# Attention and token mixer on one core: a rewrite around token halves, with four-byte transposes of fp16 pairs and four-quadrant values products

## The chip, the cores and the metric

The kernel runs on 1 core of one Trainium2 chip. The metric is the device time of one execution in microseconds (us). Most figures are medians of a few executions; a profile is one profiled execution, whose "span" runs from the first to the last instruction. An execution counts as "slow" when it is over 1.5% above the fastest of the same kernel. Ratios below are the mean time of one kernel's fast runs over the mean of the other's fast runs of the same rounds, so they are not quite the ratios of the medians quoted beside them. One "point" is 1% of the time of the kernel before, about 1.94 us.

## The reference

Inputs q, k, v are 8 batches x 8 heads x 576 tokens x 64, fp32. Each batch goes through three parts:

```
coarse:  q_d, k_d, v_d = means over 4 tokens;  softmax(q_d k_d' / 8) v_d, each row repeated 4 times
local:   softmax over |i-j| < 4 of (q k' / 8), times v
x     =  coarse + local, heads side by side: 576 x 512
mixer:   wq = x w_q ; wk = x w_k ; M2 = wk' x / 8 ; mixed = wq M2 ; out = relu(mixed) w_out
```

The kernel never forms the 576 x 576 matrix of the mixer: it computes M2 (64 x 512) first.

## The kernel before

The batches are software-pipelined. One iteration runs the parts of three batches in a fixed order; TensorE works through them while ScalarE and VectorE empty PSUM, GpSimd casts and sums, and SyncE issues every load and store. PSUM is a ring of three 2-bank tiles (`ps`) and one of two 1-bank tiles (`psm`). Names in the profile: `pv` values means, `psc` local scores, `pav` local scores times values, `pm` M2, `pmx` and `pmr` the product with M2, `pcs` coarse scores, `pca` coarse times values, `pq`, `pk`, `pr` transposes of q, k and their last rows, `po` the output product, `pol` its last 64 rows, `px`, `pod` transposes of x and the coarse result, `pw`, `pws`, `pwk` the projections and their rearrangements.

```
def load_v(b):                                    # 10 loads of 128 KB per batch
    v32 = ... [128, NW, H, D] fp32
    for n in range(NW):                           # NW = 5 windows, two of 64 tokens each
        for c in range(2):
            sp.dma_start(v32[64*c:64*c+64, n],
                         _ap(v[b], K0[2*n+c]*D, [[D, 64], [S*D, H], [1, D]]))

def tr(key, dst):                                 # q and k: 16 two-byte transposes each
    for j in range(NP):
        for f in range(4):
            pe.transpose(p_[...], t_[:, f, 2*j:2*j+2, :], id16)
    evac(dst, ..., p_...)                         # 128 x 2048 fp16, ScalarE

def av(n):                                        # two quadrants: token half c -> rows and columns 64c
    for s_ in range(2):
        for hh in range(NP):
            for c in range(2):
                pe.matmul(p_[64*c:64*c+64, ...], E[64*c:64*c+64, ...], v16[64*c:64*c+64, n, h, :],
                          tile_position=(64*c, 64*c))
    dve.reciprocal(rz[:, n], ...); dve.tensor_tensor(x_, p_, rz, op=ALU.mult)

def m2():                                         # 7 matmuls of 512 columns
    ...
    evac("M2", M2[0:64], p_[0:64], scale=s_mix)   # ScalarE; rows 64 to 127 stay zero

def mx(i):                                        # two 2-bank tiles, and mxr for the last 64 tokens
    for rr in range(2):
        r = 2*i + rr
        pe.matmul(p_[:, rr, :], M2[:, 128*r:128*r+128], wT[:, 0:512], start=True, stop=True)
    evac("mx%d" % i, ..., p_, relu=True)

ORDER = [ ... (0, "av0"), (-1, "m2"), (0, "av3"), (0, "score2"), (0, "av1"), (-1, "mx0"), (0, "av2"),
    (0, "cs0"), (-1, "mx1"), (0, "cs1"), (0, "av4"), ..., (-1, "mxr"), (1, "tq"), (0, "ca0"),
    (2, "load_v"), (-1, "og0"), (0, "ca1"), (1, "tk"), (1, "tr"), (-1, "ol"), (0, "xt0"), (0, "xt1"), ... ]
# ... cut: casts, sums, scores, coarse attention, projections, stores
```

The softmax here doesn't subtract the row's maximum and nothing guards it: scores larger than these inputs give would overflow.

## Time and profile before

| | before |
|---|---|
| time, 2 runs | 193.12 us median (192.64 and 193.6) |
| span of the profile, mean granted TensorE clock | 192.7 us, 0.950 |
| steady period (one batch) | 19.30 us, clock 1.00 |
| TensorE busy in it | 18.52 us |
| VectorE, ScalarE, GpSimd busy in it | 12.3, 13.2, 13.6 us |

The page of the profile. The first line is busy time and share by engine; PEclk is the granted TensorE clock in tenths of full speed (9 stands for 90% or more), in 40 slices of the span; DMA is the busy share of the 16 DMA engines in tenths.

```profile
span 192.7 us, 6374 instructions
PE 155.5 (81%) x2720; PEld 104.0 (54%) x2720; DVE 114.8 (60%) x286; ACT 110.7 (57%) x140; POOL 107.7 (56%) x122
...
PEclk9999555999789999999999999999999999999997
DMA  5999999899899799967999899969996943004215
...
q1 hardware_dynamic: 73920, 40.12, 81.7%
```

From the eighth slice on the clock is whole but for three slices (0.7 or 0.8), and the DMA engines are busy almost throughout until the loads end. A steady batch, from one values product to the next (columns: length of the stretch, busy us and instructions of each engine, clock, DMA share, GB/s):

```profile
core 0: us, PE busy (x) PEld busy (x) DVE busy (x) ACT busy (x) POOL busy (x), PEclk, DMA share, GB/s
...
102.04:121.34 19.30, 18.52 (x341) 12.43 (x340) 12.32 (x29) 13.22 (x18) 13.58 (x13) 1.00 0.92 245
```

TensorE is busy for 96% of it. The timeline of TensorE in that batch (start, length, engine, output and inputs, shape, count; in brackets the idle time ahead and who ended it):

```profile
102.04 0.39 PE L27 MATMUL pv<-v_1_149,P_153 128*32 128x512 f16 x1
...
105.07 0.39 PE L27 MATMUL pm_2266<-od_1955,wk_221 112*128 112x512 f16 x1
...
107.93 0.59 PE L27 MATMUL pmx<-wT_219,M_1_223 128*128 128x512 f16 x2 [0.41 <-ACT E_0_135 L27]
...
109.09 0.30 PE L27 MATMUL pcs<-qd,kd_127 64*128 64x144 f16 x4 [0.20 <-DVE x_2330 L27]
...
110.62 0.45 PE L27 MATMUL pav<-v_1_149,E_0_135 64*64 64x65 f16 x16 [0.17 <-ACT Ec_2356 L27]
...
111.20 1.05 PE L27 MATMUL pq_2408<-id_67,q_2110 128*128 128x128 f16 x16
...
112.55 1.89 PE L27 MATMUL po<-wo_91,rmx_227 128*128 128x512 f16 x8
...
114.75 1.06 PE L27 MATMUL pk_2480<-id_67,k_2111 128*128 128x128 f16 x16
115.64 0.39 PE L27 MATMUL pr<-id_67,r_2112 128*128 128x128 f16 x4
```

Three marks cut the batch into stretches: `pv` to `pm` 3.03 us, `pm` to `pq` 6.13, `pq` to the next `pv` (121.34) 10.14. The idle gaps are short: 0.41, 0.20 and 0.17 us. The next view is SyncE, which holds the issuing queue of all loads and stores (length of an issue, not of its transfer):

```profile
69.95 0.44 SPq L27 DMA_DIRECT2D q_1237<-in_q_dram  x1
70.89 1.27 SPq L27 DMA_DIRECT2D k_1238<-in_k_dram  x1
72.26 2.40 SPq L27 DMA_DIRECT2D r_1239<-in_q_dram  x1
74.71 2.23 SPq L27 DMA_DIRECT2D r_1239<-in_k_dram  x1
77.04 11.80 SPq L27 DMA_DIRECT2D v_1497<-in_v_dram  x10
88.94 0.57 SPq L27 DMA_DIRECT2D out_dram<-os  x1
```

The 17 issues of a batch take about 20 us.

### The profile page before, as it was taken

How to read it: one execution, taken by the hardware profiler on the slowest of the kernel's cores; microseconds unless marked ns; L12 is line 12 of the kernel's file. 1: busy time of each engine (PE TensorE's matmuls, PEld its weight loads, DVE VectorE, ACT ScalarE, POOL GpSimd, SP SyncE). 2: the span in 40 equal slices, each digit the busy share in tenths (PEclk: the TensorE clock that was granted, in tenths of full speed). 3: DMA queues.
4: the chain of work that ended last, by engine and by line, in shares of the span. 5: the costliest groups of instructions: out<-in, count | busy, mean ns of one | idle time of the engine just before them, and what ended most of it. 6: DMA issues, size and time to landing. Idle time of an engine off the chain costs nothing.

```text
span 192.7 us, 6374 instructions
## 1 busy us (share of the span) xinstructions
PE 155.5 (81%) x2720; PEld 104.0 (54%) x2720; DVE 114.8 (60%) x286; ACT 110.7 (57%) x140; POOL 107.7 (56%) x122
## 2 busy tenths in 40 slices
PE   0034448885899989998999899989998999898790
PEld 0034227853576647664776476647764776465330
DVE  6263978754646566656665666566656665685220
ACT  2037134954565767576757675767576757633422
POOL 5701991099748991895479547954895476000000
PEclk9999555999789999999999999999999999999997
DMA  5999999899899799967999899969996943004215
GB/s 175 314 187 215 348 290 162 191 354 175 175 319 218 174 264 294 263 137 201 278 323 156 184 280 346 187 154 296 330 215 154 300 146 112 3 3 153 93 57 188
DMA packets 74027, 40.54 MB, mean 210 GB/s; under 512 B 52432, under 2 KB 68880, under 8 KB 74000
## 3 DMA queue, kind: packets, MB, share of 16 engines
q1 hardware_dynamic: 73920, 40.12, 81.7%
q8 instruction: 21, 0.34, 0.7%
q14 instruction: 6, 0.05, 0.1%
q10 hardware_dynamic: 80, 0.03, 0.1%
HBM read 30.67 MB, written 9.44 MB: 208 GB/s over the span
## 4 chain that ended last, share of the span: by engine, by line
PE 68%; DVE 17%; ACT 7%; issue 4%; POOL 2%; ACTq 0%; DVEq 0%
PE po L27 15%; PE psc L27 6%; PE pav L27 5%; PE pw L27 4%; PE px L27 4%; PE pca L27 4%; PE pol L27 4%; DVE kd_127 L27 3%; PE pv L27 2%; PE pcs L27 2%; ACT kT L27 2%; PE pod L27 2%; DVE rz L27 1%; PE pws L27 1%; PE pwd L27 1%
## 5 line engine op out<-in xcount | busy, mean ns | idle before, releaser
L27 ACT COPY os<-po 128x1024 f32<-128x1024 f32 x16 | 16.2, 1012 | 14.7 <-issue 8.3
L27 DVE RECIPROCAL rz<-pav 128x8 f32<-128x8 f32 x40 | 8.1, 204 | 13.4 <-PE pav L27 13.4
L27 PE MATMUL po<-wo_91,rmx_227 128*128 128x512 f16 x64 | 15.3, 379 | 0.6 <-ACT rmx_227 L27 0.6
L27 PE MATMUL po<-wo_91,rmx_212 128*128 128x512 f16 x64 | 15.1, 379 | 0.0
L27 DVE COPY xT<-px 128x928 f16<-128x928 f16 (+1 forms) x32 | 13.8, 451 | 0.6
L27 PE MATMUL pq_236<-id_67,q_229 128*128 128x128 f16 x16 | 1.9, 312 | 12.6 <-DVE q_229 L27 12.6
L27 PE MATMUL psc<-id_67,neg 64*128 64x232 f16 (+1 forms) x80 | 9.4, 278 | 2.8 <-DVE vblk_201 L27 2.8
L27 PEld LDWEIGHTS <-rmx_227 128*128 128x128 f16 x80 | 7.2, 98 | 8.1 <-ACT rmx_227 L27 0.7
L27 PE MATMUL psc<-qT,kT 64*64 64x58 f16 (+1 forms) x640 | 11.4, 198 | 0.0
L27 PEld LDWEIGHTS <-rmx_212 128*128 128x128 f16 x80 | 7.2, 98 | 6.6
L27 DVE RECIPROCAL rc<-pca 128x8 f32<-128x8 f32 (+1 forms) x16 | 3.4, 211 | 11.8 <-PE pca L27 11.8
L27 PEld LDWEIGHTS <-wqk_90 128*128 128x128 f16 x96 | 8.3, 98 | 3.7 <-issue 0.9
L27 PEld LDWEIGHTS <-kT 64*64 64x64 f16 x640 | 8.7, 113 | 2.1 <-issue 2.1
L27 ACT COPY odT<-pod 128x448 f16<-128x448 f16 (+1 forms) x16 | 5.6, 402 | 6.3 <-PE pod L27 6.3
L27 PE MATMUL pw<-xT,wqk_90 128*128 128x288 f16 x64 | 9.2, 286 | 0.0
L27 PEld LDWEIGHTS <-q_229 128*128 128x128 f16 x16 | 1.6, 146 | 12.6 <-DVE q_229 L27 12.6
L27 POOL CAST v_0_147<-v_79 128x2560 f16<-128x2560 f32 x1 | 3.1, 3129 | 9.3 <-DMA w_92<-in_moe_w_k_dram 9.3
L27 DVE TENSOR_TENSOR wT_219<-pw,wTd 128x576 f16<-128x576 f32 x4 | 3.0, 758 | 8.6 <-ACT wTd L27 8.6
L27 DVE COPY ol<-pol 64x512 f32<-64x512 f32 x8 | 5.5, 682 | 4.3 <-PE pol L27 4.3
L27 DVE TENSOR_TENSOR wT_204<-pw,wTd 128x576 f16<-128x576 f32 x4 | 3.0, 758 | 8.0 <-ACT wTd L27 6.6
L27 DVE TENSOR_SCALAR rmx_227<-pmx 128x1024 f16<-128x1024 f32 x4 | 4.9, 1224 | 4.1 <-PE pmx L27 4.1
L27 POOL CAST v_1_149<-v_255 128x2560 f16<-128x2560 f32 x1 | 2.3, 2323 | 8.6 <-DMA v_255<-in_v_dram 8.6
(542 smaller groups left out, 540.9 us busy)
## 6 DMA issues: line engine op xcount, KB each, us to landing
out_dram<-os SPq DMA_DIRECT2D x16, 512.0 KB, 4.4
v_79<-in_v_dram SPq DMA_DIRECT2D x10, 128.0 KB, 4.6
v_255<-in_v_dram SPq DMA_DIRECT2D x10, 128.0 KB, 5.4
v_583<-in_v_dram SPq DMA_DIRECT2D x10, 128.0 KB, 3.5
v_1024<-in_v_dram SPq DMA_DIRECT2D x10, 128.0 KB, 4.4
v_1497<-in_v_dram SPq DMA_DIRECT2D x10, 128.0 KB, 3.6
v_1970<-in_v_dram SPq DMA_DIRECT2D x10, 128.0 KB, 4.3
v_2443<-in_v_dram SPq DMA_DIRECT2D x10, 128.0 KB, 3.4
```

The source lines that it names most:

```text
L27: return lambda *a, **k: self._tc.keep_in_program_order(f_(*a, **k))
```

## The change

The intent is to take work from TensorE. Tokens are laid out by halves (288 + 288). q and k come in as 18 whole rows per partition, are cast into fp16 pairs, and a pair is transposed as one fp32 element: 18 transposes instead of 36. v is split by head parity on the partition halves, so that the local values product can use all four 64 x 64 quadrants of the array (sixteen of its matmuls took 0.38 us before and about 0.25 after). M2 is copied to both partition halves so that the product with it runs on two row tiles at once, in four pieces. The last 64 rows of two batches share one output product. Two things less visible change as well: the fp16 copy of v has two buffers instead of three, and the two `rmx` tiles become one with two halves.

```diff
 def load_qk(b):
-    # q, k: [[4*D, 128], [S*D, H], [1, 4*D]] each, and two loads of the last 64 rows
+    for src, nm in ((q[b], "q32"), (k[b], "k32")):
+        sp.dma_start(t, _ap(src, 0, [[18*D, 128], [4*S*D, 2], [1, 18*D]]))
 def load_v(b):
     for n in range(NW):
         for c in range(2):
-            sp.dma_start(v32[64*c:64*c+64, n], _ap(v[b], K0[2*n+c]*D, [[D, 64], [S*D, H], [1, D]]))
+            for g in range(2):
+                sp.dma_start(v32[64*g:64*g+64, n, c],
+                             _ap(v[b], (g*S + K0[n][c])*D, [[D, 64], [2*S*D, 4], [1, D]]))
 def tr(key, dst):
-    (16 transposes of 128x128 fp16)
+    t_ = g_[key].bitcast(FP32)
+    for f in range(8):
+        pe.transpose(p_[...], t_[:, f].rearrange("p u e s -> p (u e s)"), id32)
 def av(n):
+    for hq in range(4):
+        for g, c in ((0, 0), (1, 1), (0, 1), (1, 0)):
+            pe.matmul(p_[64*c:64*c+64, g, ...], E[64*g:64*g+64, ...], v16[64*g:64*g+64, n, c, hq, :],
+                      start=True, stop=True, tile_position=(64*g, 64*c))
 def m2():
     evac("M2", M2[0:64], p_[0:64], scale=s_mix)
+    dve.tensor_copy(M2[64:128], M2[0:64])
-def mx(i): two 2-bank tiles of two 512-column matmuls, and mxr
+def mx(r): four 2-bank tiles
+    for c in range(2):
+        pe.matmul(p_[:, c, 0:HS], M2[64*c:64*c+64, 128*r:128*r+128], wT[64*c:64*c+64, c, 0:HS], ...)
 def ol():
+    if b % 2 == 0: return
+    (128 rows: the last 64 of one batch and the first 64 of the next)
-ORDER: ... av1, mx0, av2, cs0, mx1, cs1, av4, mxr, tq ...
+ORDER: ... av1, mx0, mx1, av2, cs0, mx2, cs1, av4, mx3, tq ...
... cut: constants, casts, sums, masks, scores, coarse attention, projections
```

## The prediction

> **What bounds it now.** Steady iterations (one batch each) last 19.30 us; the busy times by stretch give PE 18.52, POOL 13.6, ACT 13.2, DVE 12.3 us in each, the DMA engines 0.86-0.93 of it, clock 1.00. The chain of waits is nearly all PE there: 16 output matmuls (po) 3.46 us, M2 (pm) 1.62, 36 two-byte transposes of q, k and remainder 2.07, x transposes 1.12, local AV 80 matmuls about 2.0 (25-28 ns each), mx+mxr 1.1, pw 0.98, pca 0.94, pol 0.86, pcs 0.7, pv 0.66. About 0.9 us is DVE and ACT work it waits for (x, Ec). Before that PE waits 12.6 us for the first q cast, then behind DVE's 7.6 us of kd/kdt adds; steady state starts near 60 us, and the last batch drains from 176 us.
>
> **What changes per iteration on PE** (estimates from the trace).
> - AV on four quadrants: the scores already run so, 32 in 0.45 us, 14 ns each. 80 x 14 = 1.2: -0.8.
> - mx with K=64, two row tiles together: four times 288 columns, 0.5 instead of 1.1: -0.6.
> - ol once for two batches: -0.43. cs: -0.3. vd on 64x32 tiles: -0.25.
> - 18 four-byte transposes for 36 two-byte ones at 56-60 ns. [...] I guess 60-110 ns each, 1.1-2.0 us: 0 to -1. No fp32 transpose stands in this trace.
> PE work falls from 18.4 to 15-16 us.
>
> **Other engines.** ACT: qT/kT eviction 1.86 us for 2048 two-byte elements becomes 1024 four-byte ones, about 1.0 like os (1.01): -1.5 in all, 11.8. DVE about even, 11.8 (merged od, xT; half of ol; plus a copy of M2 and mx in two pieces). POOL: casts 2 x (2 x 1152) elements into 4-byte-strided halves, about 4.4-5.5 us (was 1.9+1.9+0.6); kd adds 160 instead of 116 elements: 14-15 us. DMA: q, k as 4608 B runs instead of 1024 and 256 B; v stays at 256 B packets in 20 half-size loads; 17.5 to about 16 us.
>
> **Critical path.** Not all 3 us come home. (a) Between av0 and ca0 PE will hold 4.5-5 us of work against DVE's 5 x 0.84 for x plus two mx evictions, about 5.8, with three PSUM buffers: DVE-bound, some 1 us lost. (b) A loop on POOL: remainder eviction -> sums -> q/k casts -> tq -> ca/og0 -> tk, tr -> eviction. Before it is 11.4 + 5.3 us with 2.6 slack; after about 12.5 + 4.7 = 17.2. I predict the loop closes: iteration about 17.2 us, PE busy some 90%.
> Seven such iterations: -15. Start: fewer constants ahead of the q cast, shorter qT/kT evictions, less kd: -5. Tail: -1. Sum: 193.1 - 21 = 172 us; I say 173, range 164 to 184. Faster by over 2%: 0.91; within 2%: 0.06; slower: 0.03.
>
> **What shows it.** Period 16.5-17.8 us; AV 15 ns apart; fp32 transposes at 60-110 ns; qT eviction near 1.0 us; PE waiting for q casts by POOL at tq, or for DVE's x tiles at PSUM buffers; ACT and DVE near 11.8 us per period; DMA share still about 0.9; first transpose near 10-11 us.
>
> **What would make it wrong.** [...] strided casts on POOL or DVE at half rate (POOL loop to 19+, little gain); 20 v loads holding the issuing queue so that v's cast comes late; or, the other way, POOL's casts not binding and the period reaching 15.7 (result near 162).

Two passages on fp32 transposes, which no trace of this case showed, are cut: a reason given ahead of the guess of 60 to 110 ns, and the first of the ways to be wrong. The guess rests on no measurement but the 56 to 60 ns of the two-byte transposes; measured afterwards: 109 ns apart, 113 on average. The sum: 15, 5 and 1 us are the 21, and 193.1 - 21 = 172; the "0 to -1" us an iteration in it rests on that guess.

## The result, and the profile after

| | before | after |
|---|---|---|
| time, 2 runs each | 193.12 us | 226.94 us (225.48 and 228.39) |
| ratio of fast runs, 95% interval | | 1.1743 [1.1549, 1.1937] |
| span, mean clock | 192.7 us, 0.950 | 223.8 us, 0.847 |
| steady period | 19.30 us | 22.2 to 25.5 us |

It became slower by 17%, where 10% faster was predicted. The page after:

```profile
span 223.8 us, 6572 instructions
PE 167.9 (75%) x2816; PEld 110.6 (49%) x2816; DVE 107.0 (48%) x260; ACT 99.1 (44%) x141; POOL 115.3 (52%) x112
...
PEclk9996558757889967997699959995899699958999
DMA  6946993597379349933998389836992474002206
...
q1 hardware_dynamic: 54464, 40.12, 62.5%
...
q8 instruction: 22, 0.36, 0.7%
```

Every engine's share fell, and so did that of the DMA engines (81.7 to 62.5%) at the same 40.12 MB: no engine has too much work, the kernel waits. The clock falls again and again all along. By stretches of TensorE's timeline the span grew 7.5 us up to the third values product (63.44 to 70.93), 20.3 us over the next five batches (96.50 to 116.77), and 3.3 us after them. One of the five batches, and then its middle in pieces of 3.4 us (columns as before):

```profile
94.45:117.41 22.96, 20.24 (x351) 13.33 (x350) 11.67 (x25) 11.58 (x18) 14.38 (x12) 0.85 0.68 194
...
99.80:103.20 3.40, 1.84 (x76) 1.12 (x65) 2.80 (x6) 1.55 (x3) 3.40 (x3) 1.00 0.31 68
103.20:106.60 3.40, 2.50 (x29) 1.69 (x30) 2.40 (x6) 2.17 (x3) 0.32 (x1) 0.61 0.44 99
106.60:110.00 3.40, 3.40 (x20) 2.10 (x19) 0.96 (x3) 1.01 (x1) 1.69 (x1) 0.50 0.89 297
```

TensorE stands idle for 1.56 of 3.40 us, and directly afterwards its clock is granted at one half. TensorE's timeline in the same batch:

```profile
94.45 0.53 PE L27 MATMUL pv<-v,Pm 64*32 64x260 f16 x24
...
97.96 0.60 PE L27 MATMUL pm<-od,wk 128*128 128x512 f16 x2
...
100.75 0.42 PE L27 MATMUL pmx<-wT,M 64*128 64x288 f16 x2 [0.60 <-ACT E L27]
101.83 0.30 PE L27 MATMUL pmx<-wT,M 64*128 64x288 f16 x2 [0.67 <-DVE x L27]
...
102.68 0.52 PE L27 MATMUL pcs<-qd,kd 64*128 64x168 f16 x12 [0.29 <-DVE x L27]
...
104.18 0.46 PE L27 MATMUL pcs<-qd,kd 64*128 64x168 f16 x4 [0.54 <-DVE x L27]
...
105.58 1.94 PE L27 MATMUL pq<-id,q 128*128 128x128 f32 x8 [0.22 <-ACT Ec L27]
...
108.21 3.15 PE L27 MATMUL po<-wo,rmx 128*128 128x512 f16 x8
...
111.66 1.07 PE L27 MATMUL pk<-id,k 128*128 128x128 f32 x8
112.57 0.27 PE L27 MATMUL pr<-id,q 128*128 128x128 f32 x1
```

The stretches are now 3.51, 7.62 and 11.83 us (were 3.03, 6.13, 10.14). In the middle one the gaps are 0.60, 0.67, 0.29, 0.54 and 0.22. In the last one `po` takes 3.15 us instead of 1.89: that is the half clock, not more work. And at full clock the eight fp32 transposes `pk` take 0.91 us to the start of `pr`, where the sixteen fp16 ones took 0.89: no gain. VectorE in the middle stretch:

```profile
100.30 0.52 DVE L27 COPY M<-M 64x512 f16<-64x512 f16 x1 [1.29 <-ACT M L27]
100.85 0.21 DVE L27 RECIPROCAL rz<-pav 128x8 f32<-128x8 f32 x1
101.09 0.69 DVE L27 TENSOR_TENSOR x<-pav,rz 128x512 f16<-128x512 f32 x1
```

VectorE takes its instructions in program order here. It stands 1.29 us until ScalarE has written M2, copies it, and only then begins on the next local result (TensorE had it ready at 99.89), whose PSUM tile TensorE needs back: the results behind the copy wait for something that has nothing to do with them. Last, SyncE's queue from the start, and in a steady batch:

```profile
1.80 17.00 SPq L27 DMA_DIRECT2D v<-in_v_dram  x20
...
22.51 20.08 SPq L27 DMA_DIRECT2D v<-in_v_dram  x20
...
110.48 19.31 SPq L27 DMA_DIRECT2D v<-in_v_dram  x20
```

The twenty loads of 64 KB take 17 to 21 us to issue in a batch, about 0.85 to 1.04 us each; the ten of 128 KB took 9.4 to 11.8. TensorE's wait for the cast of v (us in total, times, longest), before and after:

```profile
PE pv L27 <- POOL v_0_147 L27: 5.2, 1, 5.2
...
PE pv L27 <- POOL v L27: 14.3, 2, 8.6
```

Before, it was 5.2 us, once. Now the first two batches stand 8.6 and 5.6 us for the cast of v, which waits for the last load of v. In the later batches TensorE does not wait for v.

### The profile page after: what moved, and what is told of

Read it like the earlier page. It is cut to its first block, busy times and chain, and to the rows that moved or that the text cites. A ratio compares the mean times of both kernels' runs of the same rounds, so it can differ in the third digit from the quotient of the medians.

```text
span 223.8 us, 6572 instructions
## 1 busy us (share of the span) xinstructions
PE 167.9 (75%) x2816; PEld 110.6 (49%) x2816; DVE 107.0 (48%) x260; ACT 99.1 (44%) x141; POOL 115.3 (52%) x112
## 3 DMA queue, kind: packets, MB, share of 16 engines
q1 hardware_dynamic: 54464, 40.12, 62.5%
## 5 line engine op out<-in xcount | busy, mean ns | idle before, releaser
L27 POOL CAST v<-v 128x2560 f16<-128x2560 f32 x8 | 18.6, 2322 | 54.6 <-DMA v<-in_v_dram 38.5
L27 PE MATMUL po<-wo,rmx 128*128 128x512 f16 x128 | 36.1, 432 | 0.1
L27 DVE TENSOR_TENSOR x<-pav,rz 128x512 f16<-128x512 f32 x40 | 27.7, 691 | 1.4
L27 POOL TENSOR_TENSOR sum<-qT 128x1152 f32<-128x1152 f16 x8 | 16.8, 2106 | 18.2 <-ACT qT L27 17.8
L27 PE MATMUL pq<-id,q 128*128 128x128 f32 x64 | 15.6, 425 | 12.3 <-DVE q L27 10.7
L27 PEld LDWEIGHTS <-rmx 128*128 128x128 f16 x144 | 14.7, 109 | 17.2 <-issue 6.9
L27 ACT ACTIVATE E<-psc 128x928 f16<-128x928 f32 (+1 forms) x24 | 19.4, 806 | 6.4 <-PE psc L27 5.7
L27 POOL CAST q<-q 128x1152 f16<-128x1152 f32 x14 | 20.2, 1488 | 0.0
L27 POOL CAST k<-k 128x1152 f16<-128x1152 f32 x14 | 20.2, 1485 | 0.0
L27 PEld LDWEIGHTS pq<-id,q 128*128 128x128 f32 x64 | 12.5, 224 | 14.0 <-DVE q L27 10.7
L27 PE MATMUL pv<-v,Pm 64*32 64x260 f16 (+1 forms) x192 | 4.9, 286 | 14.3 <-POOL v L27 14.3
L27 POOL TENSOR_TENSOR sum<-kT 128x1152 f32<-128x1152 f16 x7 | 14.7, 2106 | 0.5
```

The source lines that it names most:

```text
L27: return lambda *a, **k: self._tc.keep_in_program_order(f_(*a, **k))
```

## The experiments

Theory Q: the issuing queue costs the most. Theory G: the copy of M2 on VectorE, and the fourfold product with M2, open the gaps in the middle stretch. Theory C: the gaps bring the half clock, which costs more than the gaps. Rival: TensorE's new work (fp32 transposes, many narrow matmuls) is simply longer. Kernels are named for what they change; "m2pe", "mx3", "fill" and "vpool2" are explained where they first occur. Edits are to the kernel after, unless said.

| kernel | result | median us | ratio to before, fast runs [95%] |
|---|---|---|---|
| copy_late | right | 229.69 | 1.1821 [1.1733, 1.1909] |
| m2pe | right | 221.9 | 1.1406 [1.1316, 1.1496] |
| v10wrong | wrong | 210.27 | 1.0834 [1.0761, 1.0908] |
| bv20 (kernel before) | right | 233.0 | 1.1996 [1.1881, 1.2111] |
| v10wrong_fill | wrong | 203.71 | 1.0539 [1.0465, 1.0613] |
| vact | right | 241.02 | none (one fast run) |
| m2pe_vact | right | 234.06 | 1.2037 [1.1946, 1.2129] |
| m2pe_vact_fill | right | 234.49 | none (one fast run) |
| v10wrong_m2pe | wrong | 206.52 | 1.0709 [1.0625, 1.0793] |
| v10wrong_mx3 | wrong | 208.56 | 1.0782 [1.0717, 1.0847] |
| v10wrong_m2pe_mx3 | wrong | 199.3 | 1.0179 [1.0073, 1.0285] |
| m2pe_mx3_vpool | right | 208.89 | 1.0756 [1.0667, 1.0845] |
| v10wrong_m2pe_mx3_fill | wrong | 193.25 | 0.99 [0.982, 0.998] |
| vpool2 | right | 214.29 | 1.1018 [1.0947, 1.109] |
| mended | right | 207.73 | 1.0575 [1.0491, 1.0659] |
| mended_fill | right | 208.88 | 1.0745 [1.069, 1.0801] |
| line_good | right | 208.7 | none (one fast run) |
| line_bad | right | 207.9 | 1.0514 [1.0393, 1.0636] |

The median of the kernel before in the rounds of these runs was 193.57 to 194.83 us.

### copy_late: the copy of M2 behind two local products

```diff
-            dve.tensor_copy(M2[64:128], M2[0:64])        # in m2
+        def m2c(): dve.tensor_copy(M2[64:128], M2[0:64])
+ORDER: ... av3, score2, av1, m2c, mx0, mx1 ...
```

> The changed kernel, with its new copy of M2 to the upper 64 partitions moved in program order from straight behind m2 to behind av3 and av1, just ahead of mx0. No work is taken away. Theory G (gaps and clock): in each iteration VectorE holds still for 1.3 us at that copy until ScalarE has written M2, then spends 0.6-0.8 us on it, and the x tiles of av3 and av1 queue behind it; PE runs out of PSUM buffers (about 2.3 us of gaps between M2 and the q transposes), and the low activity drops the granted clock to 0.50 for the 6.8 us that follow. Then the gaps fall to about 1 us, the clock stays at 1.00 in most iterations, the period falls from about 23.3 to 19-20.5 us and the time from 227 to 200-210. Rival Q (issuing queue): the 20 value loads of a batch hold the issuing queue for 17-20 us of each period and set it; then the period stays within 1 us of 23.3 and the time over 220.

Measured 229.69 us, ratio 1.1821, within the interval of the change itself, as rival Q had said (over 220). Theory G failed in this form: the wait moved, it did not go. TensorE now waited 9.3 us in seven batches, up to 1.7 each, for the copy at `pmx`. Late or early, the copy lies on the path.

### m2pe: M2 made on both halves by TensorE, no copy

```diff
-                pe.matmul(p_, w_[i], t_, start=(j == 0), stop=(j == NW+1))
+                for o in (0, 64):
+                    pe.matmul(p_[o:o+64], wk[:, i], t_, start=(j == 0), stop=(j == NW+1),
+                              skip_group_check=True, tile_position=(0, o))
-            evac("M2", M2[0:64], p_[0:64], scale=s_mix)
-            dve.tensor_copy(M2[64:128], M2[0:64])
+            evac("M2", M2, p_, scale=s_mix)
```

> The changed kernel, with M2 made twice by TensorE (64-column weights at column tiles 0 and 64, side by side) and evicted once over 128 partitions, so that VectorE's copy of M2 is gone. Theory G: as copy_late or 1 to 4 us better (0.6 us less VectorE work and one hop less ahead of mx), 197-208. If column tiles of 512 columns do not run side by side, M2 takes 3.2 instead of 1.6 us and the gain shrinks by up to 1.6 us per iteration. Rival Q: over 220.

Measured 221.9 us, ratio 1.1406: about 3 points better than the change, far from the 197 to 208 of theory G, and again over 220 as rival Q had said. The column tiles do run side by side: in a sample batch the 14 matmuls of M2 took 1.63 us, where the 7 of the kernel before took 1.61. The stretch keeps gaps of 0.61, 0.57, 0.48, 0.22 and 0.42 us in a sample batch: now the four `pmx` tiles and their evictions hold the PSUM ring.

### v10wrong: ten loads of v, with wrong rows

The right ten loads would need four dimensions (head parity, token, head, element), where each load of these kernels has three; no run tried one. So this kernel reads 128 tokens in a row and gives a wrong result; bytes, runs of 256 B and everything downstream stay the same.

```diff
-                for g in range(2):
-                    sp.dma_start(v32[64*g:64*g+64, n, c], _ap(v[b], (g*S + K0[n][c])*D, [[D, 64], [2*S*D, 4], [1, D]]))
+                sp.dma_start(v32[:, n, c], _ap(v[b], K0[n][c]*D, [[D, 128], [2*S*D, 4], [1, D]]))
```

> The changed kernel with 10 value loads per batch in place of 20, same bytes, same 256-byte runs, 128 partitions each; half of the values are the wrong tokens, so the result is wrong on purpose. Rival Q: the queue's 24 us per period fall to about 14, period 18-19 us, time 190-200. Theory G: only the first two batches, where PE waited 8.6 and 5.6 us for values, gain: about 5-9 us, time 217-223, period still about 23 us with the clock at 0.50 in the same place.

Measured 210.27 us, ratio 1.0834: 9 of the 17 points are gone, some 17.6 us at 1.94 us a point. That lies between the stakes (190 to 200 for Q, 217 to 223 for G), and the steady period came out at about 22 us, nearer to G's 23 than to Q's 18 to 19. The third values product starts at 61.44 us instead of 70.93, since TensorE's wait for v is now

```profile
PE pv L27 <- POOL v L27: 5.0, 1, 5.0
```

instead of 14.3 us. The five steady batches take 110.60 instead of 116.77 us, although TensorE waits for v in none of them in either kernel. Of these 6.2 us, 3.8 are busy time of TensorE (97.82 instead of 101.62; the clock is 0.92 in three of the five batches instead of one, and 0.85 to 0.87 in the others), and 2.1 are one pause for instructions that v10wrong does not have (see line_good). So the number of issues is the largest single part, as theory Q has it; it acts as a wait for v at the start, but in the steady batches only by way of the clock and of that pause. Why the queue moves those two is not shown.

### bv20: the kernel before with twenty loads of v

```diff
-                sp.dma_start(v32[64*c:64*c+64, n], _ap(v[b], K0[2*n+c]*D, [[D, 64], [S*D, H], [1, D]]))
+                for g in range(2):
+                    sp.dma_start(v32[64*c:64*c+64, n, 4*g:4*g+4],
+                                 _ap(v[b], (4*g*S + K0[2*n+c])*D, [[D, 64], [S*D, 4], [1, D]]))
```

> The kernel before with each of its 10 value loads of a batch split by heads into two (20 of 64 KB), right result. If an issue costs about 0.85-0.95 us whatever its size, the queue needs about 26 us per batch, and the time goes from 193 to 225-240 us: then Q is a limit by itself and would also cap a mended changed kernel at about 20-22 us a batch. If the 0.9 us is only the drain of the bytes (the 10 loads of double size took 1.03 us each), nothing changes beyond 3%: 190-199 us.

Measured 233.0 us, ratio 1.1996. Nothing but the number of issues (and so the size of each) was changed, and the kernel before became as slow as the change (the intervals overlap). Its twenty issues take 15.7 to 17.2 us a batch. The longest of TensorE's waits in it:

```profile
PE pv L27 <- POOL v L27: 31.9, 7, 8.6
```

Seven batches wait for v, 31.9 us together. The number of issues is a cost by itself, in both kernels.

### v10wrong_fill: dead matmuls in the gaps

Ten dead 512-column matmuls per batch, whose result nobody reads, keep TensorE busy where it waits.

```diff
+        def fill(n):
+            p_ = psm(name="pfl")
+            for _ in range(n): pe.matmul(p_, wo16[:, 0, 0:128], wo16[:, 1, :], start=True, stop=True)
+ORDER: fill 3, 3, 1, 2, 1 times before mx0, mx1, cs0, cs1, tq        # on top of v10wrong
```

> v10wrong (so the issuing queue is not the limit; wrong result on purpose) with ten dead 512-column matmuls added per batch where PE waits between M2 and the q transposes (into a PSUM bank of their own, read by nobody): 2.2 us more PE work per batch. Theory G2 (PE is quicker than the evictions there, its activity drops, and the granted clock is 0.50 for the next 6.8 us, worth 3.4 us per batch): the 0.50 stretches go, the period falls from 22.2 to 19-20 us, time from 210 to 190-198 though work was added. Rival C (the clock drops because of what runs there, K=64 tiles and four-byte transposes, or costs nothing): 0.50 stays or nothing is gained, time 209-225.

Measured 203.71 us, ratio 1.0539: 3 points better than v10wrong, 6.6 us where 12 to 20 were expected. The clock of its page:

```profile
PEclk9997558999999999999999999999999999999996
```

It is 1.00 in all five steady batches (v10wrong: 0.85 to 0.92). More work on TensorE made it faster: theory C. But the batch is still 21.3 us: the fill itself is 2.2 us (ten at 0.216), and `pm` to `pq` takes 8.1 to 8.6 us (v10wrong: 7.5 to 8.3).

### vact, m2pe_vact, m2pe_vact_fill: half of v's loads issued by ScalarE

```diff
+ (0, c == 1 loads) two at a time on act.dma_start, after og0, ca1, tr, xt1, odt     # sp keeps c == 0
```

> The changed kernel with 10 of the 20 value loads of a batch issued by ScalarE's queue, spread over the iteration; right result. Theory Q (20 issues on one queue cost about 17 of the 33 us, most of it in the first two batches): 208-216 us, first values product of batch 1 at about 40 instead of 46.7 us, period about 22-23; ScalarE gets some 5 us of issuing per batch, which may cost part of it. Theory without Q: 224-230.

> m2pe (M2 written twice by TensorE, 222) and vact together, right result. If both parts act on different limits, the gains add: 200-210 us. If the low clock remains in the period, not below 200.

> m2pe_vact with the ten dead matmuls of v10wrong_fill; right result. Theory G2: clock 1.00 in the steady part, period 18.5-20 us, 188-197 us: about as quick as the kernel before. Rival C: as m2pe_vact or up to 15 us slower.

Measured 241.02 (one fast run, 235.09), 234.06 and 234.49 us (one fast run, 228.84): the first two are worse than the change, the last is level with it at best, and all missed what was expected. An issue takes 0.63 to 1.0 us there and stands in ScalarE's own order; in vact's profiled run, a slow one, ScalarE stood 16.1 us behind loads of v before it emptied `odT`. These runs neither support theory Q nor refute it, since the issues held ScalarE up; with that, the other two parts could not be read from them.

### v10wrong_m2pe, v10wrong_mx3, v10wrong_m2pe_mx3: the two parts of the middle stretch

mx3 goes back to the earlier shape of the product with M2: two 2-bank tiles and a remainder.

```diff
-        def mx(r): four 2-bank tiles of 2 x 288 columns
+        def mx(i): two 2-bank tiles, rows 2i and 2i+1, 256 tokens of each half
+        def mxr(): the last 32 tokens of each half, in two 1-bank tiles
-ORDER: ... av1, mx0, mx1, av2, cs0, mx2, cs1, av4, mx3, tq
+ORDER: ... av1, mx0, av2, cs0, mx1, cs1, av4, mxr, tq
```

> v10wrong (issuing queue out of the way, wrong on purpose, 210) with M2 made twice by TensorE as in m2pe. Theory H (VectorE standing still at the copy of M2 is what stretches the stretch from M2 to the q transposes from 6.15 us before to 7.8-8.1): that stretch falls to 6.5 or less, gaps under 1 us, clock back, 190-198 us. Theory R (the ring of three PSUM buffers: twelve tiles instead of ten pass through it there, since mx became four): it falls only by the 0.5 us of the copy, to 7.2-7.6, and the time to 204-208.

> v10wrong with mx packed again as before: two rows of 256 tokens per half in one PSUM tile (two tiles in the ring instead of four) and the last 32 tokens of each half in the two single-bank buffers outside the ring; K=64 row tiles stay, and so does the copy of M2. Theory R: the stretch from M2 to the q transposes falls to 6.3-6.9, low clock rarer, 195-203 us. Theory H: 207-211 us.

> v10wrong with both. If each is part of the cause: the stretch near 6.0 us as in the kernel before, the clock at 1.00 in the steady part, a period of 18.5-19.5 us, 185-194 us, no better than level with the kernel before because the work saved on PE is small. If neither: above 203.

Measured 206.52, 208.56 and 199.3 us (of the last, two runs were slow; the fast ones took 195.77 and 198.15), ratios 1.0709, 1.0782 and 1.0179. Alone the parts give 1.2 and 0.5 points over v10wrong (the second is within the noise), together 6.5; each alone came out where the other's theory had put it, and both together missed the 185 to 194. Either alone leaves the ring of PSUM tiles blocked by the other: with the copy gone TensorE waits 4.0 us for ScalarE's evictions of `pmx`, with the tiles gone 8.9 us for VectorE's local results. In the profiled run of the third (a slow run) `pm` to `pq` is 6.29 us in two of five steady batches (before 6.13), and 6.9 to 7.8 in the others.

### m2pe_mx3_vpool: a part of the loads from GpSimd, with a right result

```diff
-                    sp.dma_start(v32[64*g:64*g+64, n, c], ...)
+                    eng = pool if c == 1 and (b < 2 or n < 2) else sp
+                    eng.dma_start(v32[64*g:64*g+64, n, c], ...)        # on top of m2pe and mx3
```

> Right result: the changed kernel with both mends, and the value loads shared with GpSimd's queue (half of them in the first two batches, 4 of 20 later). The issuing queue is left with 16 loads, about 14 us, plus 4-5 us for the rest: 18-19 us per batch. If an issue costs GpSimd about 1 us as it costs the others, it has room for 4: 192-202 us. If GpSimd's issues are dearer or hold its casts up: 205-225.

Measured 208.89 us, ratio 1.0756. Ten of its issues came ahead of GpSimd's constants, so in its profiled run (a slow one) the first transposes of q waited 19.3 us instead of 10.7. A fault of this kernel, mended below.

### v10wrong_m2pe_mx3_fill: all three causes taken away

> v10wrong_m2pe_mx3 (199, wrong on purpose) with seven dead 512-column matmuls per batch (1.5 us at full clock) in the gaps that remain ahead of mx0, cs0 and av4. If the 0.50 clock after those gaps is what is left of the cause: clock 1.00 in the steady part, period 19.0-19.8 instead of 21.2, 186-193 us. If the clock is a symptom only: 199-206.

Seven dead matmuls per batch on top of v10wrong_m2pe_mx3. Measured 193.25 us, ratio 0.99: level with the kernel before. The clock of its page:

```profile
PEclk9999556999999999999999999999999999999997
```

Queue, middle stretch and clock together make up the whole loss. They leave little of a gain: three steady batches take 20.51 us each on average, of which the seven dead matmuls at 0.216 are at most 1.5 (partly they fill idle time), so 19.0 or more (an estimate) against 19.30.

### vpool2, mended, mended_fill: the same with right results

vpool2 issues from GpSimd the ten c = 1 loads of the first batch, after its constants, and 4 of 20 for each later batch. mended is vpool2 with m2pe and mx3; mended_fill adds the seven dead matmuls.

> The changed kernel, right result, with part of the value loads on GpSimd's queue: 10 of 20 for batch 0 (after GpSimd's constants), 4 of 20 for the others. Queue theory: the first values product at about 20 instead of 23.4 us, the second at about 42 instead of 46.7, so 5 us at the start; the steady period, bound by gaps and clock, 22-23: 214-221 us. Without the queue as a cause: 225-230.

> Right result: M2 by TensorE twice, mx in two tiles and a rest, and the loads of vpool2. Queue at 18-19 us a batch, stretch from M2 to the q transposes 6.3 us at full clock: 196-204 us, some low clock left.

> mended with the seven dead matmuls. Clock theory: 188-197 us, 5 to 9 below mended. Clock a symptom: as mended or up to 8 slower.

Measured 214.29, 207.73 and 208.88 us; ratios 1.1018, 1.0575 and 1.0745. vpool2 confirms theory Q with a right result: 7 points. mended missed its expectation. The fill brought the clock from 0.90 to 0.96 and did not help: that is what "clock a symptom" had staked, so theory C is shown only for the kernels with wrong rows. Here the pauses described next grew, from some 8 us to 13 in the profiled runs. Steady batches of mended:

```profile
84.61:103.28 18.67, 16.82 (x366) 11.80 (x365) 10.95 (x23) 11.87 (x19) 16.26 (x16) 1.00 0.66 189
103.28:127.50 24.22, 20.73 (x371) 13.83 (x371) 11.59 (x24) 11.99 (x19) 17.88 (x18) 0.86 0.83 218
```

```profile
112.13 0.25 PE L27 MATMUL pav<-v,E 64*64 64x65 f16 x6 [2.35 <-issue]
```

One batch takes 18.67 us, the next 24.22. In the second TensorE pauses 2.35 us in the midst of sixteen equal matmuls; "issue" means that it waits for nothing the profile shows. Its mean clock is 0.86, against 1.00 in the first. mended_fill has 13 us of such pauses in all, the longest 3.3.

### line_good, line_bad: where TensorE's own instructions come from

The list of DMA packets in the trace has a queue named "instruction" with packets of 16,384 B, 21 to 24 per run. That is one for each 256 instructions of TensorE (21 for 5,455 in the kernel before, 22 for 5,652 in the change). I set the pauses against them and against TensorE's own count of instructions (weight loads, matmuls, and 15 to 27 semaphore and drain instructions):

```
kernel       pause, us          count mod 256   last instruction packet ahead of its end
before       46.19 to 48.52     193             45.65 to 46.99
after       120.51 to 122.64    193            119.68 to 121.28
mended      109.78 to 112.13    193            108.97 to 110.49
mended_fill 155.74 to 159.07    193            156.46 to 157.78
```

A count over all 18 traces taken by then gives 46 pauses over 0.25 us in 15 of them (v10wrong, vact and m2pe_vact have none): all stand at the same count modulo 256, and end 1.2 to 1.7 us after the end of such a packet. Two kernels then moved the block ends (a block is 256 instructions from one such count to the next), by tiny dead matmuls; they differ from each other in nothing but the number at the start:

```diff
+        def pad(): 18 dead matmuls (14 for odd b) of 32x16, ahead of mx0      # 768 TensorE instructions per batch
+    58 such dead matmuls at the start in line_good, 95 in line_bad             # on top of mended
```

> In nine traces all 25 pauses of the TensorE that the profile marks 'issue' and that are longer than 0.25 us lie at one place modulo 256 in TensorE's own instruction count (193 of 256), and end 1.3 to 1.7 us after a 16 KB packet of the queue named 'instruction'. Theory I: TensorE then waits for its next 256 instructions[...]. This kernel is the mended one with 18 or 14 tiny dead matmuls per batch, so that each batch has 768 TensorE instructions, and 58 at the start, so that a block ends about 220 and 476 instructions after the values product, which cuts the dense stretch in two halves of some 5 us each. Theory I: no such pause over 0.3 us in the steady periods from the third batch on; time 195 to 204 us (mended 207.7). Rival D (the pauses come of the full load queue, wherever the blocks lie): pauses as in mended, 4 to 7 us in sum, time 205 to 212.

Theory I had a time for a block below which the pause was to come. It was not shown: in the kernel before, the block ahead of the pause was worked off in 4.2 us, but two blocks of 4.00 us had no pause behind them.

> The same kernel and the same instructions per batch, but 95 dead matmuls at the start instead of 58, so that a block ends about 146 and 402 instructions after the values product: the 256 of the densest 3.6 us make one block. Theory I: a pause of 1 to 3 us at the end of that block, among the local values products, in most steady periods, all at the same place of the count modulo 256; time 210 to 224 us and over 8 us above line_good. Rival D: the same time as line_good within 2 us.

The pauses of line_bad:

```profile
115.01 0.22 PE L27 MATMUL pav<-v,E 64*64 64x65 f16 x3 [3.08 <-issue]
...
138.25 0.22 PE L27 MATMUL pav<-v,E 64*64 64x65 f16 x4 [1.68 <-issue]
...
160.96 0.22 PE L27 MATMUL pav<-v,E 64*64 64x65 f16 x4 [3.36 <-issue]
```

Half of theory I held. All eight pauses of the two kernels stand at 193 modulo 256 again; in line_bad they moved to one place of the batch (398 to 400 instructions after the values product), as expected. But line_good has pauses too (1.35, 1.78 and 3.73 us in steady batches), and the times are alike: 208.7 and 207.9 us, with one fast run of the first (205.31) and two of the second (202.36 and 204.8). That is what rival D expected. Both profiled runs were slow ones, so only the places are read from them.

What goes with a pause is how late the packet starts. In all 20 traces, in blocks with one such packet, its start lies a median of 1.1 us after TensorE enters the block where the DMA engines' share in between (from 1 us ahead) is under 0.8 (136 blocks), and 2.6 us where it is over (185 blocks, the middle half of them 1.6 to 3.5). The longest pause of line_good shows the sum: TensorE enters the block at 150.80, the packet starts 5.15 us later, at 155.94 to 157.19, and its instructions are used 1.55 us after that, at 158.74; the block ahead of them had been worked off in 4.2 us, so TensorE stood 3.7. That the pause is a wait for the next 256 instructions is shown by the places; that the packet comes late because of the loads is a correlation, and no run took the loads away.

## Why the prediction was wrong

- **The step that failed most**: "v stays at 256 B packets in 20 half-size loads; 17.5 to about 16 us". The loads were priced by bytes. The queue that issues them was not priced, though "20 v loads holding the issuing queue" stood among the ways to be wrong. An issue of 64 KB held it 0.85 to 1.04 us, nearly as long as one of 128 KB (0.94 to 1.18), so v's issues grew from about 11 to 17 to 21 us of a batch. Undoing it alone gives back 9 of 17 points (v10wrong), 9.5 us of it ahead of the third batch, where TensorE waits for v; doing it alone to the kernel before costs 20% (bv20), where TensorE waits 31.9 us for v.
- **(a), "some 1 us lost"** between av0 and ca0: mis-sized. The middle stretch grew by 1.5 us in place of shrinking, by the copy of M2 in VectorE's order and by four 2-bank tiles in a ring of three. The two overlap: 1.2 and 0.5 points alone, 6.5 together. Even with both gone TensorE waits about 1.8 us there (mended).
- **A step that was missing**: the clock. The sum took full speed for granted. The gaps of (a) bring a half clock for the transposes of q, the coarse product and the first half of the output product: that stretch grew by 1.7 us a batch. In the trace after, the clock was 0.50 for 6.83 us (103.94 to 110.77) directly after 3.41 us with 1.62 us idle, and five of the six such stretches between 80 and 203 us are as long; with gaps of 0.8 us a batch in the kernel before, and with 1.85 us in a batch of mended, it stayed at 1.00. How much idle time brings the half clock was not shown. Filling the gaps is worth 3 points (v10wrong_fill; the same again with the other two causes gone), and nothing in mended_fill.
- **"PE work falls from 18.4 to 15-16 us"**: mis-sized. In two steady batches of mended without a pause and at clock 1.00, TensorE is busy 17.68 and 16.82 us, 17.25 on average, from 18.52: 1.3 us less instead of 2.4 to 3.4. And it idles 1.85 us in each of them (0.78 before), nearly all in the middle stretch, behind ScalarE's `E` and `Ec` and VectorE's `rz`. So waits take 1.1 us of the 1.3 back, and 0.2 us came home (19.10 against 19.30). The fp32 transposes came at the end of the guessed range, 109 ns apart and 113 on average with the slower first of a group, where the gain is zero: 18 at 113 ns are 2.03 us, 36 at 56 ns 2.02. The local product did go from 0.38 to about 0.25 us for sixteen matmuls (15 ns apart, as predicted), but VectorE's 0.9 us per result sets the pace there. `pv` saves 0.19 us and `pws`, now 17 narrow matmuls instead of 8, gives 0.4 back. The joined last rows save 0.86 us every second batch.
- **(b), GpSimd's loop**: it did not bind. Its casts take 5.9 to 6.0 us a batch for q and k (predicted 4.4 to 5.5), and its sums stood 17.8 us in all waiting for ScalarE's q.
- **Right**: the eviction of q, 1.012 us (about 1.0 predicted); ScalarE and VectorE at 11.6 and 12.1 us a batch (11.8); the first transposes at 10.7 us (10 to 11). Not right: the DMA share, 0.56 to 0.81 in the steady batches (about 0.9).
- **Why a mended kernel does not win**: mended has batches of 18.67 and 19.53 us without and with the joined rows where nothing disturbs, 19.1 on average against 19.30. The pauses for instructions, some 8 us in its profiled run, take more than that back.

In sum, at 1.94 us a point: issuing queue 9.1 points (17.6 us), middle stretch 6.5 (12.6 us), the rest of the half clock 2.8 (5.4 us), which is 18.4 of 17.4 and leaves a gain of 1 point. The parts come from rounds on different chips, each against the kernel before, in kernels with wrong rows, and hold for this order of taking them away: with the queue still in place the copy of M2 alone gave 3 points (m2pe), and part of the queue's share came by way of the clock.

Open: why an issue of 64 KB of v holds the queue 0.85 to 1.04 us while one of 1152 KB of q or k holds it 0.41 to 1.2. The time is not a fixed one: in mended, where GpSimd issues 4 of the 20, SyncE's 16 still take 15.6 to 19.4 us, 0.97 to 1.2 each. Open too is whether shorter code for the dense stretch, or fewer loads in flight around it, would end the pauses. No kernel here with a right result beats the one before.

## What to carry to other kernels

Price a transfer twice, by its bytes and by the time its issue holds the queue (here 0.85 to 1.04 us for a 64 KB load of v, against a median of 2.9 us from issue to landing); a layout that splits each transfer in two doubles the issues (bv20: 20% slower). A saving on TensorE is worth what the neighbours' evictions allow, and a new hop in their order of work (a copy, two more PSUM tiles) can cost more than it, once directly and once more through the clock (here 1.5 us a batch in the middle stretch, and 1.7 in the one behind it, where the clock was 0.50). Many tiny matmuls are also many instructions: in line_good TensorE worked off 256 instructions in 4.2 us, the packet with the next ones started 5.15 us after it had entered them, and it stood 3.7 us.
